# Row maxima of a block by four transfers for sixteen, and denominators inverted three steps later, in a mixed linear and softmax attention kernel

## The chip, the cores and the metric

One core of one Trainium2 chip runs the whole program. The metric is the device time of one execution in microseconds, the median of several runs.

## The reference

Two attention layers over the same input, mixed by a gate. Layer A is linear attention with a learned softmax feature map, layer B is ordinary softmax attention without a mask. There are 2048 tokens, a model width of 448, and 16 heads of 28.

```
q, k, v = split(x @ B_wqkv)                        # layer B
scores  = q @ k.T * 28 ** -0.5                     # 2048 x 2048 for each head
b = concat_heads(softmax(scores) @ v) @ B_wo
phi(u) = [softmax(u @ w_phi), softmax(-u @ w_phi)] # layer A
a = concat_heads(phi(q) (phi(k).T v) / (phi(q) sum(phi(k)) + 1e-6)) @ A_wo
g = sigmoid(sum(x * gate_w))
out = g * a + (1 - g) * b                          # all in fp32
```

The change concerns layer B, the softmax attention.

## The kernel before, in words

**Stages.** The first 360 us or so project q and k, compute layer A and the values of layer B, and begin the row maxima. After that comes the attention loop, 256 steps (`for s in range(NS + 18)`). The 16 heads lie in 4 groups of 4 (`g`), the queries in 4 ranges of 512 (`qb`). A block `gq = 4 * g + qb` is one group with one query range, and it takes 16 steps, one for each tile of 128 keys (`kt`). A step has 12 score matmuls (4 heads in 4 row strips of the TensorE array, 3 passes with high and low halves of q and k), 4 exponentials on ScalarE (L839) and, two steps later (`LAG`), 4 value matmuls (L976) that add into the one PSUM bank `pv`. Three more matmuls a step (L288) compute scores of later blocks for their row maxima, and VectorE reduces each of them (L295). Seven PSUM banks go round among these; the VectorE reduction of a step has to be done before its banks can be written again.

**Row maxima.** The softmax subtracts each query's maximum inside the score matmul. The query stack `qst` has, for each head, 32 partitions: row 32h holds the maxima, the 28 rows from 32h + 4 hold q. The key stack has -1 in that row. `mx_reduce` (L223) reduces a block's partial maxima to `red`, turns it in 32 x 32 squares on VectorE to `nm` (L234), and `load_nm` (L812) brings `nm` to the four rows of `qst` by small transfers (L817). `load_q` (L808, L804) brings q itself by four transfers. There are two query stacks, so those of block `gq + 2` can be filled when block `gq` has made its last scores.

**Denominators.** The values carry a column of ones, so row 32j + 28 of `pv` holds the denominators of head j. `finish` (L1012) works after a block's last step in parts that are listed by step in `late`:

- `f1`: VectorE copies `pv` to `oU` (L373), and SP spreads the denominators over 128 partitions, `den` (L376);
- `f2`: VectorE inverts them (L383), SP writes them to HBM, `rd` (L387), and reads them back broadcast over 32 partitions, `rs` (L388);
- `f3`: GpSimd multiplies `oU` by `rs` (L394); `f4`: it splits the result in two halves, `oT` (L402, L403);
- `f5`: SP stores `oT` to HBM (L1033) for the output projection. In the last group the projection reads `oT` itself (`project`, at the steps in `PROJ`).

`oU`, `oT` and `rs` have one buffer each here, `den` has two.

**Order.** The instructions of TensorE, VectorE, ScalarE and GpSimd stand in the order in which the program writes them. Those of SP, which issues every DMA, are put in order by the scheduler, by when it reckons them ready, and then run in that order: a transfer that waits holds up all behind it. SP often takes the loads of a stack long before the step that writes them down.

The names and lines below are those of the kernel before.

Of the kernel before, what the change touches and what calls it, by code (L numbers as in the profile page):

```python
# [8 lines left out]
F32 = mybir.dt.float32  # L9
F32R = mybir.dt.float32r  # L10
# [7 lines left out]
P = 128  # L18
# [5 lines left out]
NG = 4  # L24
# [12 lines left out]
def f32(ap):  # L37
    return ap.bitcast(F32)
# [3 lines left out]
def gated_mix_kernel(ctx, tc, xT, wqkB, wvB, wvA, wkAT, wqAT, phi, woA, woB,  # L42
# [7 lines left out]
    nc = tc.nc  # L50
# [5 lines left out]
    mxp = ctx.enter_context(tc.tile_pool(name="mxp", bufs=2))  # L56
# [100 lines left out]
    nm_of = {}  # L157
    acts = []
    subs = []
    part = mxp.tile([P, NU * 4], F32, name="part", bufs=1)  # L160
    nc.gpsimd.memset(part, LOWEST)
    red = mxp.tile([P, 32], F32R, name="red", bufs=1)
    nc.vector.memset(f32(red), 0.0)

    def take_acts():
# [57 lines left out]
    def mx_reduce(gq):  # L223

        col = 64 * gq
        n = 2 if gq < GM else 4

        def reduce():
            nc.vector.tensor_reduce(
                red[:, :16].rearrange("p (h t) -> p h t", t=4),  # L230
                part[:, col:col + 16 * n].rearrange("p (k t h) -> p h t k", t=4, h=4),
                AX.X, ALU.max)
            nm_of[gq] = nm = mxp.tile([P, 32], F32, tag="nm", name=f"nm{gq}", bufs=7)
            nc.vector.transpose(nm, f32(red))  # L234

        mxs["fin"].append(reduce)
# [132 lines left out]
    def normalize1(pool, pn, nm, n):  # L369

        oU = pool.tile([P, n, 512], F32, tag="oU", name=f"oU{nm}", bufs=2 * n - 1)
        for i in range(n):
            (nc.scalar.copy if n == 2 else nc.vector.tensor_copy)(oU[:, i, :], pn[i])  # L373
        den = pool.tile([P, n, 16], F32, tag="den", name=f"den{nm}", bufs=2)
        for i in range(n):
            nc.sync.dma_start(den[:, i, :], oU[DH:P:32, i, :])  # L376
        return oU, den

    def normalize2(pool, oU, den, nm, n, eps):

        if eps:
            nc.vector.tensor_scalar_add(den, den, EPS)
        nc.vector.reciprocal(den, den)  # L383
        rd = dr.tile([4, n * 512], F32, tag=f"rd{n}", name=f"rd{nm}", bufs=2)
        rs = pool.tile([P, n, 512], F32, tag="rs", name=f"rs{nm}", bufs=n)
        for k in range(n):
            nc.sync.dma_start(rd[:, k * 512:(k + 1) * 512], den[:, k, :])  # L387
        nc.sync.dma_start(rs.rearrange("p n q -> p (n q)"),  # L388
                          rd.unsqueeze(1).to_broadcast([4, 32, n * 512]))
        return oU, rs  # L390

    def normalize3(oU, rs, n):

        (nc.gpsimd if n == 1 else nc.vector).tensor_mul(oU, oU, rs)  # L394
        return oU

    def normalize4(pool, oU, nm, n):

        oTn = []
        for k in range(n):  # L400
            oT = pool.tile([P, 2, 512], F32R, tag="oT", name=f"oT{nm}_{k}", bufs=3 * n - 2)
            (nc.scalar.copy if n == 2 else nc.gpsimd.tensor_copy)(oT[:, 0, :], oU[:, k, :])  # L402
            nc.gpsimd.tensor_sub(oT[:, 1, :], oU[:, k, :], f32(oT[:, 0, :]))  # L403
            oTn.append(oT)
        return oTn
# [275 lines left out]
    for i in range(2 * NT + 11):  # L681
        t, q = i, i - NT
# [107 lines left out]
    qst_of, kst_of = {}, {}  # L790
# [20 lines left out]

    def load_nm(gq):  # L812
        nm = nm_of.pop(gq)
        for h in range(4):
            row = f32(qst_of[gq][32 * h:32 * h + 1, 0, :].rearrange("p (t b r) -> p t b r", b=4, r=32))
            for b in range(4):
                nc.sync.dma_start(row[:, :, b, :], nm[32 * b + 4 * h:32 * b + 4 * h + 4, :])  # L817

    def load_k(g, kb):
        kst_of[(g, kb)] = load_stack(kst[(4 * g + kb) % 5], k_d[g], kb * 512)  # L820
# [2 lines left out]
    pv_of, pts, late, mids = {}, {}, {}, {}  # L823
# [64 lines left out]
    stg = at  # L888
    load_q(0)
    load_nm(0)  # L890
    rlp = fr_s.enter_context(tc.tile_pool(name="rlp", bufs=1, reuse_waits="tile"))
    mx_unit()
# [88 lines left out]
    def project(qb, oT, tl):  # L981

        t = qb * 4 + tl
        acc = acc_of[qb][:, tl, :]
        po = take_bank(f"pob{t}")
        run(po[:, :D], first_passes(qb, tl) + out_passes(oT, tl * P, woB_s, NG - 1))
        nc.vector.scalar_tensor_tensor(acc, po[:, :D], gate1[:, t:t + 1], acc,  # L987
                                       op0=ALU.mult, op1=ALU.add)
        nc.sync.dma_start(out[0, t * P:(t + 1) * P, :], acc)
# [22 lines left out]
    def finish(gq, s):  # L1012

        st = {}
        g, qb = divmod(gq, NQ)
        last = gq == NG * NQ - 1

        def f1():
            st["n"] = normalize1(late_p, [pv_of[gq]], f"b{gq}", 1)

        def f2():
            st["n"] = normalize2(late_p, *st["n"], f"b{gq}", 1, False)

        def f3():
            st["n"] = normalize3(*st["n"], 1)

        def f4():
            st["o"], = normalize4(late_p, st["n"], f"b{gq}", 1)

        def f5():  # L1030
            for j in range(4):
                r = (4 * g + j) * DH
                nc.sync.dma_start(o_d[r:r + DH, :, qb * 512:(qb + 1) * 512],  # L1033
                                  f32(st["o"][32 * j:32 * j + DH]))

        if last:
            finish_last(gq)
            return
        copies.append(f1)
        late.setdefault(s + 3, []).append(f2)  # L1040
        late.setdefault(s + 7, []).append(f3)
        late.setdefault(s + 8, []).append(lambda: acts.append(f4))
        if g < NG - 1:
            late.setdefault(s + 13, []).append(f5)
        else:
            for tl in range(4):
                mids[PROJ[qb] + tl] = lambda tl=tl: project(qb, st["o"], tl)
# [57 lines left out]
    for s in range(NS + 18):  # L1105
        gq, kt = divmod(s, NT)
        g, qb = divmod(gq, NQ)
        take_acts()
        if s < NS:
            if s in (0, 3):  # L1110
                load_k(0, 2 + s // 3)
            if g + 1 < NG and qb == NQ - 1 and kt in (2, 7):
                load_k(g + 1, kt // 4)
            if g and qb == 0 and kt in (0, 2):
                load_k(g, 2 + kt // 2)
            if kt == 5 and gq + 1 < NG * NQ:
                load_q(gq + 1)
            if kt == (12 if gq + 1 < 14 else 14) and gq + 1 < NG * NQ - 1:
                load_nm(gq + 1)
            if s in OUTS:  # L1120
                load_out(OUTS.index(s))
            if g == NG - 1 and kt == (12 if qb < 2 else 14):
                load_acc(qb)
# [8 lines left out]
        while vals and vals[0] <= upto:  # L1132
            t = vals.pop(0)
            values(t)
            if t % NT == NT - 1:
                finish(t // NT, s)
        take_copies()
        mx_fin()
        if NG * NQ - 1 in nm_of and NG * NQ - 1 in qst_of:
            load_nm(NG * NQ - 1)  # L1140
# [70 lines left out]
```

## Time and profile before

| | us |
|---|---|
| median of 3 runs (lowest, highest) | 1004.69 (1003.24, 1008.66) |
| the profiled execution: time | 1004.62 |
| its span | 1002.8 |
| TensorE busy | 987.7 |
| ScalarE busy | 752.8 |
| VectorE busy | 725.6 |
| GpSimd busy | 234.2 |

The span runs from the first to the last instruction of the program; the other 1.8 us of the execution lie around it. [...] In the rows of a timeline stand the start and the duration in microseconds, the engine, the line and the operation, what it writes and reads, how many of them are merged in the row, and in square brackets the idle time before and what ended it. SPq is SP's queue of DMA issues: the duration there is that of the issue, not of the transfer. In the rows of waits stand the total, how often, and the longest.

### The profile page before, as it was taken

The numbers are of one execution on the slowest core, as the hardware profiler recorded it, in microseconds if no ns is written. First come the engines' busy times: TensorE is split into PE (matmuls) and PEld (weight loads), VectorE is DVE, ScalarE is ACT, GpSimd is POOL, SyncE is SP. The second block draws the span as 40 slices with busy tenths as digits, with TensorE's granted clock in tenths as the row PEclk, the third lists the DMA queues.
The fourth block names the chain that finished last, engine by engine and source line by source line (L and its number), as shares of the span: only waits on it lengthen the run. The fifth ranks groups of instructions, "written<-read, shape, count | busy, mean of one in ns | idle before, by whom it ended". The sixth has DMA issues, their size and how long they took to land.

```text
span 1002.8 us, 22531 instructions
## 1 busy us (share of the span) xinstructions
PE 987.7 (98%) x8392; PEld 604.5 (60%) x8392; DVE 725.6 (72%) x1335; ACT 752.8 (75%) x1442; POOL 234.2 (23%) x224
## 2 busy tenths in 40 slices
PE   9999999999999999999989999999999999999998
PEld 8877777877877655445544455545454555555555
DVE  5566777898765778888867888878877887885112
ACT  4455556587765789888878888898887888987662
POOL 1134544679634700201101101101011011100010
PEclk9999999999999999999999999999999999999999
DMA  8973010122233134211122121122221122100441
GB/s 305 313 236 111 32 53 32 43 57 79 80 105 103 64 117 137 51 47 49 49 85 67 41 60 43 46 76 79 68 81 40 50 75 73 31 20 12 148 156 56
DMA packets 56909, 84.49 MB, mean 84 GB/s; under 512 B 17984, under 2 KB 24752, under 8 KB 56800
## 3 DMA queue, kind: packets, MB, share of 16 engines
q1 hardware_dynamic: 56800, 83.06, 26.8%
q8 instruction: 66, 1.08, 0.4%
q14 instruction: 43, 0.35, 0.1%
HBM read 54.86 MB, written 27.78 MB: 82 GB/s over the span
## 4 chain that ended last, share of the span: by engine, by line
PE 86%; DVE 6%; DMA 3%; SPq 2%; issue 1%; ACT 1%; POOL 1%; DVEq 0%; POOLq 0%; ACTq 0%
PE g L831 27%; PE pv L976 24%; PE pqk L109 4%; PE pk L127 4%; PE poa L109 4%; PE pva L127 4%; PE g L288 3%; PE pob L109 3%; PE pmd L260 3%; PE pvb L127 2%; DVE part L295 2%; SPq L817 2%; DMA denb<-oUb 2%; PE pvb L109 1%; PE pq L109 1%
## 5 line engine op out<-in xcount | busy, mean ns | idle before, releaser
L839 ACT ACTIVATE p<-g 128x512 f32<-128x512 f32 x1020 | 526.1, 607 | 101.2 <-PE g L831 101.0
L295 DVE TENSOR_REDUCE part<-g 128x1 f32<-128x512 f32 x704 | 441.6, 682 | 82.9 <-PE g L288 80.5
L831 PEld LDWEIGHTS g<-qst,kst 32*128 32x128 f32 x3060 | 221.2, 184 | 226.9 <-DVE part L295 207.4
L831 PE MATMUL g<-qst,kst 32*128 32x512 f32 x3060 | 345.5, 423 | 8.9 <-DVE part L295 8.1
L976 PE MATMUL pv<-p,vb 128*32 128x512 f32 x2048 | 274.5, 608 | 0.0
L288 PE MATMUL g<-kc,qc 28*128 28x512 f32 x704 | 233.3, 496 | 0.5
L394 POOL TENSOR_TENSOR oUb<-oUb,rsb 128x512 f32<-128x512 f32 x15 | 19.3, 1285 | 526.5 <-DMA rsb<-rdb 314.5
L265 DVE CUSTOM_DVE_ANT_0 rl<-pmb,rl 128x512 f32<-128x512 f32 x160 | 103.2, 682 | 44.4 <-ACT rl L264 44.4
L264 ACT ACTIVATE rl<-pmd 128x512 f32<-128x512 f32 x160 | 87.3, 601 | 31.2 <-PE pmb L260 28.3
L288 PEld LDWEIGHTS g<-kc,qc 28*128 28x128 f32 x704 | 87.0, 183 | 3.0 <-DVE part L295 2.6
L976 PEld LDWEIGHTS pv<-p,vb 128*32 128x32 f32 x2048 | 40.6, 108 | 68.5 <-issue 67.3
L109 PE MATMUL pqk<-XH,wB 128*128 128x512 f32 x192 | 59.3, 397 | 0.0
L987 DVE SCALAR_TENSOR_TENSOR acc<-pob,gate,acc 128x448 f32<-128x448 f32 x12 | 8.2, 684 | 54.2 <-PE pob L109 54.2
L546 ACT CAST ev<-pqk 128x512 fp32r<-128x512 f32 x28 | 16.0, 588 | 37.5 <-PE pqk L109 23.9
L109 PE MATMUL poa<-woA_s,oTa 128*128 128x448 f32 x192 | 43.4, 375 | 0.0
L260 PE MATMUL pmb<-kp,qp 28*128 28x512 f32 x160 | 42.3, 493 | 0.5
L109 PEld LDWEIGHTS pqk<-XH,wB 128*128 128x128 f32 x192 | 35.3, 188 | 8.9 <-issue 1.5
L547 DVE TENSOR_TENSOR ev<-pqk,ev 128x512 fp32r<-128x512 f32 x28 | 19.0, 689 | 29.2 <-ACT ev L546 29.0
L260 PE MATMUL pmd<-kp,qp 28*128 28x512 f32 x160 | 40.0, 495 | 0.0
L127 PE MATMUL pk<-wkA_s,XH 128*128 128x448 f32 x128 | 39.4, 382 | 0.0
L109 PEld LDWEIGHTS poa<-woA_s,oTa 128*128 128x128 f32 x192 | 34.9, 188 | 6.3 <-issue 2.9
L127 PE MATMUL pva<-wvA_s,XH 128*128 128x450 f32 x128 | 37.8, 371 | 0.0
(154 smaller groups left out, 1084.5 us busy)
## 6 DMA issues: line engine op xcount, KB each, us to landing
qkd<-ev SPq DMA_DIRECT2D x28, 512.0 KB
qst<-qkd SPq DMA_DIRECT2D x64, 112.0 KB
kst<-qkd SPq DMA_DIRECT2D x64, 112.0 KB
od<-oTb SPq DMA_DIRECT2D x48, 112.0 KB
rsa<-rda SPq DMA_DIRECT2D x8, 512.0 KB
qst<-nm SPq DMA_DIRECT2D x256, 0.5 KB
oL<-od SPq DMA_DIRECT2D x8, 512.0 KB
rsb<-rdb SPq DMA_DIRECT2D x15, 256.0 KB
```

The lines of the kernel that those rows point to most:

```text
L109: nc.tensor.matmul(dst, l, r, start=i == 0, stop=i == len(todo) - 1)
L127: nc.tensor.matmul(dst[:, :n], l, r, start=i == 0, stop=i == len(todo) - 1, skip_group_check=True)
L260: nc.tensor.matmul(pm[j], qc[js, qt * P:(qt + 1) * P], kc[js, :], start=True, stop=True, tile_position=(32 * i, 0))
L264: nc.scalar.activation(rl, pm[i], AF.Relu)
L265: nc.vector.tensor_tensor_reduce(rl, pm[2 + i], rl, 1.0, LOWEST, ALU.add, ALU.max, part[:, col + i:col + i + 1])
L288: nc.tensor.matmul(pm, mxs[("qc", gq)][js, qt * P:(qt + 1) * P], mxs[("kc", gq // NQ, kb)][js, :], start=True, stop=True, tile_position=(3 ...
L295: nc.vector.tensor_reduce(part[:, col:col + 1], pm, AX.X, ALU.max)
L394: (nc.gpsimd if n == 1 else nc.vector).tensor_mul(oU, oU, rs)
L817: nc.sync.dma_start(row[:, :, b, :], nm[32 * b + 4 * h:32 * b + 4 * h + 4, :])
L831: nc.tensor.matmul(st[j], kst_of[(gq // NQ, kt // 4)][js, k, (kt % 4) * P:(kt % 4 + 1) * P], qst_of[gq][js, q, :], start=n == 0, stop=n == ...
L839: nc.scalar.activation(p, st[j], AF.Exp, scale=SCALE)
L976: nc.tensor.matmul(pv[32 * j:32 * j + 32, :], vb[kt // 8][:, kt % 8, 4 * g + j, :], pt[j], start=kt == 0, stop=kt == NT - 1, tile_position ...
```

## The change

The transposed maxima get another layout. `red` becomes 128 columns wide: the four maxima of tile t of the query range stand in columns 32t to 32t + 3, one for each head, and the other columns stay zero. The transpose then turns four squares of 32 columns, and a head's maxima of a 32-query square come to lie in one partition, 32b + h, for all four tiles. Four transfers, one for each square row b, bring four partitions each to the rows 0, 32, 64 and 96 of the query stack; there were sixteen, one for each head and square row. Each transfer moves 16 runs of 128 bytes, where it moved 4.

In `finish`, the steps `f2`, `f3` and `f4` come three steps later, except for the last two blocks, and `f5` comes two steps later.

```
-    red = mxp.tile([P, 32], F32R, name="red", bufs=1)
+    red = mxp.tile([P, 128], F32R, name="red", bufs=1)
...
             nc.vector.tensor_reduce(
-                red[:, :16].rearrange("p (h t) -> p h t", t=4),
-                part[:, col:col + 16 * n].rearrange("p (k t h) -> p h t k", t=4, h=4),
+                red.rearrange("p (t c) -> p t c", t=4)[:, :, :4],
+                part[:, col:col + 16 * n].rearrange("p (k t h) -> p t h k", t=4, h=4),
                 AX.X, ALU.max)
-            nm_of[gq] = nm = mxp.tile([P, 32], F32, tag="nm", name=f"nm{gq}", bufs=7)
+            nm_of[gq] = nm = mxp.tile([P, 128], F32, tag="nm", name=f"nm{gq}", bufs=7)
             nc.vector.transpose(nm, f32(red))
...
     def load_nm(gq):
         nm = nm_of.pop(gq)
-        for h in range(4):
-            row = f32(qst_of[gq][32 * h:32 * h + 1, 0, :].rearrange("p (t b r) -> p t b r", b=4, r=32))
-            for b in range(4):
-                nc.sync.dma_start(row[:, :, b, :], nm[32 * b + 4 * h:32 * b + 4 * h + 4, :])
+        row = f32(qst_of[gq][0:P:32, 0, :].rearrange("h (t b r) -> h t b r", b=4, r=32))
+        for b in range(4):
+            nc.sync.dma_start(row[:, :, b, :], nm[32 * b:32 * b + 4, :].rearrange("h (t r) -> h t r", t=4))
...
         copies.append(f1)
-        late.setdefault(s + 3, []).append(f2)
-        late.setdefault(s + 7, []).append(f3)
-        late.setdefault(s + 8, []).append(lambda: acts.append(f4))
+        by = 3 if g < NG - 1 or qb < 2 else 0
+        late.setdefault(s + 3 + by, []).append(f2)
+        late.setdefault(s + 7 + by, []).append(f3)
+        late.setdefault(s + 8 + by, []).append(lambda: acts.append(f4))
         if g < NG - 1:
-            late.setdefault(s + 13, []).append(f5)
+            late.setdefault(s + 15, []).append(f5)
```

## The prediction

> **What bounds the kernel now.** I read the page first, for the busy shares and the chain of waits.
>
> ```profile
> PE 987.7 (98%) x8392; PEld 604.5 (60%) x8392; DVE 725.6 (72%) x1335; ACT 752.8 (75%) x1442; POOL 234.2 (23%) x224
> ```
>
> ```profile
> PE 86%; DVE 6%; DMA 3%; SPq 2%; issue 1%; ACT 1%; POOL 1%; DVEq 0%; POOLq 0%; ACTq 0%
> ```
>
> TensorE is the bound, but the chain leaves it: it passes through DVE, a DMA and SP's queue, and those are the two things the diff edits. So the second view is the timeline of TensorE, for the pace of the attention steps. A step begins its value matmuls with one row of L976; these are the rows of step 0, step 208 and step 224 (blocks 0, 13 and 14).
>
> ```profile
> 362.76 1.07 PE L976 MATMUL pv<-p,vb 128*32 128x512 f32 x8
> ```
>
> ```profile
> 859.54 1.07 PE L976 MATMUL pv<-p,vb 128*32 128x512 f32 x8
> ```
>
> ```profile
> 896.31 1.07 PE L976 MATMUL pv<-p,vb 128*32 128x512 f32 x8
> ```
>
> Block 13 takes 896.31 - 859.54 = 36.77 us, 2.298 us a step. At that pace the 14 blocks from 362.76 would take 14 x 36.77 = 514.8 us; they take 896.31 - 362.76 = 533.55. So 18.8 us are lost in them somewhere. The third view, the waits, says where DVE stood.
>
> ```profile
> DVE denb L383 <- DMA denb<-oUb: 20.8, 12, 6.0
> ```
>
> ```profile
> SPq L1033 <- POOL oTb L403: 74.2, 10, 8.0
> ```
>
> The reciprocal of the denominators waits 12 times, 20.8 us in all, for the small transfer denb. That is the size of the loss. (The second row, SP's own, is used below.) The fourth view is the worst case, the denominators of block 3, inverted in block 4: first SP's queue, then DVE, POOL and TensorE in the same stretch.
>
> ```profile
> 482.20 3.56 SPq L804 DMA_DIRECT2D kst<-qkd  x4
> 485.86 0.47 SPq L387 DMA_DIRECT2D rdb<-denb  x1
> 488.24 0.58 SPq L388 DMA_DIRECT2D rsb<-rdb  x1
> 496.89 3.37 SPq L1033 DMA_DIRECT2D od<-oTb  x4
> 500.36 6.96 SPq L804 DMA_DIRECT2D kst<-qkd  x8
> 507.42 6.12 SPq L176 DMA_DIRECT2D kc<-qkd  x12
> 513.64 3.50 SPq L804 DMA_DIRECT2D qst<-qkd  x4
> 517.18 4.75 SPq L817 DMA_DIRECT2D qst<-nm  x7
> 522.04 0.60 SPq L376 DMA_DIRECT2D denb<-oUb  x1
> ```
>
> ```profile
> 481.60 0.25 DVE L383 RECIPROCAL denb<-denb 128x16 f32<-128x16 f32 x1 [0.86 <-DMA denb<-oUb]
> ...
> 511.01 0.69 DVE L373 COPY oUb<-pv 128x512 f32<-128x512 f32 x1
> ...
> 523.95 0.25 DVE L383 RECIPROCAL denb<-denb 128x16 f32<-128x16 f32 x1 [6.02 <-DMA denb<-oUb]
> ```
>
> ```profile
> 493.55 1.28 POOL L394 TENSOR_TENSOR oUb<-oUb,rsb 128x512 f32<-128x512 f32 x1 [36.05 <-DMA rsb<-rdb]
> 494.90 0.61 POOL L402 CAST oTb<-oUb 128x512 fp32r<-128x512 f32 x1
> 495.59 1.28 POOL L403 TENSOR_TENSOR oTb<-oUb,oTb 128x512 fp32r<-128x512 f32 x1
> ```
>
> ```profile
> 519.23 1.07 PE L976 MATMUL pv<-p,vb 128*32 128x512 f32 x8
> ...
> 527.57 1.94 PE L976 MATMUL pv<-p,vb 128*32 128x512 f32 x8
> ...
> 531.24 1.06 PE L976 MATMUL pv<-p,vb 128*32 128x512 f32 x8
> ```
>
> The copy that feeds denb is done at 511.7, but SP issues denb only at 522.04, behind query loads and seven of the sixteen row transfers; it lands 1.91 us later. DVE has reached the reciprocal at 523.95 - 6.02 = 517.93 and holds the next steps' L295 reductions behind it, these hold the PSUM banks, and TensorE has no bank to score into: two steps take 531.24 - 519.23 = 12.01 us in place of 4.60, so this one wait costs 7.4 us.
>
> Part of that is the clock. Windows over this place and over a shorter gap in block 10 (the third column from the right is the granted clock), then TensorE's gap and two step rows of block 10:
>
> ```profile
> 524.00:528.00 4.00, 3.20 (x19) 1.61 (x23) 3.49 (x7) 1.11 (x3) 0.00 (x0) 0.51 0.03 5
> 753.70:757.30 3.60, 3.42 (x26) 1.03 (x27) 3.01 (x5) 1.80 (x4) 0.00 (x0) 0.85 0.12 35
> 757.30:760.40 3.10, 3.10 (x27) 1.37 (x23) 1.98 (x3) 1.64 (x4) 0.62 (x1) 0.62 0.13 46
> ```
>
> ```profile
> 753.70 0.50 PE L831 MATMUL g<-qst,kst 32*128 32x512 f32 x2 [1.66 <-DVE part L295]
> ```
>
> ```profile
> 755.79 1.57 PE L976 MATMUL pv<-p,vb 128*32 128x512 f32 x8
> 759.30 1.20 PE L976 MATMUL pv<-p,vb 128*32 128x512 f32 x8
> ```
>
> After the stall the clock falls to 0.51, and in block 10 to 0.62, where the step after the wait takes 759.30 - 755.79 = 3.51 us, 1.21 over pace. I count it to the wait and let it go with it.
>
> **The change part by part.** *Sixteen row transfers become four.* The old ones (four runs of 128 bytes each) cost SP 4.75 / 7 = 0.68 us apiece, 10.9 us a block. A new one moves four times as many runs. The nearest rows: kc, 28 runs, 6.12 / 12 = 0.51 us; qst, 56 longer runs, 3.50 / 4 = 0.88 us. So issue time hardly follows the runs; I take 0.68, 2.7 us a block, with 0.51 as lower end and 4 x 0.68 = 2.7 us each (proportional to runs) as upper end. SP is nobody's bound, so the 8.2 us saved count only through denb. The rows land a block ahead of use, so nothing waits for them sooner or later.
>
> *Where denb then stands.* In the built program SP's order is: query loads (4), rows (4), denb, in most blocks; in block 4 two qc loads come between, in block 8 four qc and one kst, in block 9 one kc. Before, eleven rows (seven in block 4) stood ahead. Block 4 again, by rows: the reciprocal of block 2's denominators has its turn at 481.60 - 0.86 = 480.74, and three steps later at 487.6; rdb goes at 488.0, rsb 2.4 later (488.24 - 485.86) at 490.4, lands 5.3 later (493.55 - 488.24) at 495.7, POOL's three operations take 496.87 - 493.55 = 3.3, to 499.0, od 3.5, to 502.5. Then four kst (the other four of the eight now stand ahead of rsb) to 506.0, twelve kc to 512.2, four qst to 515.8, four rows to 518.5, two qc to 519.5, denb lands at 521.4.
>
> *The reciprocal three steps later.* Its turn moves from 517.93 by 6.9 to 524.8, or 524.0 if block 3's wait of 0.86 goes too. So even here denb is 2.6 us early, and elsewhere by more. The waits on denb go to none; what is late next is nothing on DVE, only TensorE's own pace of 2.298. Term: -18.8 us.
>
> *What moves with it.* POOL's multiply, cast and subtraction (steps 7 and 8 to 10 and 11), rdb and rsb after the reciprocal, and the four od stores. They hide behind POOL's idle time (36.05 us ahead of the multiply). The buffer oU must be free at the next block's copy, 511.01; it is free at 499.0, some 11 us early. Project steps (qb 0 and 1) come 24 and 16 steps after a block's end; block 14 isn't moved. Cost 0.
>
> *The wider transpose and reduction.* Sixteen of each:
>
> ```profile
> L229 DVE TENSOR_REDUCE red<-part x16: 129/252/266, 111.2 to 918.2; 128x16 fp32r<-128x64 f32 x11, 128x16 fp32r<-128x32 f32 x5
> L234 DVE STREAM_TRANSPOSE nm<-red x16: 211/211/214, 111.5 to 918.5; 128x32 f32<-128x32 f32 x16
> ```
>
> The reduction handles the same elements: 0. The transpose takes 128 columns for 32: between 0 and 3 x 0.211 = 0.63 us more. Nearest is the copy, 0.69 / 512 = 1.35 ns a column: 96 x 1.35 = 0.13 us. In the attention steps that is hidden, since DVE takes a whole copy of 0.69 without TensorE losing a step:
>
> ```profile
> 398.28 0.69 DVE L373 COPY oUb<-pv 128x512 f32<-128x512 f32 x1
> ```
>
> ```profile
> 399.47 1.07 PE L976 MATMUL pv<-p,vb 128*32 128x512 f32 x8
> ```
>
> ```profile
> 401.74 1.06 PE L976 MATMUL pv<-p,vb 128*32 128x512 f32 x8
> ```
>
> (The step right after the copy: 2.27 us.) The five of the earlier stage I count in full, 5 x 0.13 = +0.65; with all sixteen at the upper end it would be +10.1.
>
> Sum: 1004.62 (the profiled execution: span 1002.8 and 1.8 around it; the median of the three runs, 1004.69, is the same within 0.1) - 18.8 + 0.65 = 986.5.
>
> [...]
>
> **The rivals.** *The slow step stays.* If the clock of block 10 fell for another reason than its gap, 1.21 us remain: 987.7. Against: the low clock begins at the gap's end, in both blocks. It lies inside the forecast's own range, and I give it 0.05.
>
> *Issue goes by runs.* At 2.7 us a row transfer, denb of block 4 lands 8.1 us later, at 529.5, 5 us behind the reciprocal, and the place costs nearly what it costs now, 7.4: 993.9. For it: 56-run loads take longer than 28-run ones. Against: 14 times the runs of an old row transfer cost 1.3 times as much.
>
> *The transpose is slow and seen*: +10.1 less 0.65, 996. Against it speaks the hidden copy.
>
> *Slower: oU is held too long.* The three steps come off its slack. If rsb landed over 11 us later than I work out, DVE's copy would wait for POOL, the one pv bank would stay full, and every later step of TensorE would wait. For it: SP blocks on L1033 for oT already (74.2 us, up to 8.0), and rdb and rsb stand behind kst loads in that in-order queue. Against: denb, the latest of these transfers, is 6.0 us late at worst now. At one step in each of 13 blocks it costs 13 x 2.3 = 29.9: 1016. It decides from 18.8 / 13 = 1.4 us of copy wait a block; around that point the result is no change, about 1005.
>
> **How the numbers follow.** A change under 0.5% (5.0 us) can't be told from none here. Forecast 0.75 (own range 984 to 990); the slow step 0.05, in the same range; issue by runs 0.08 and transpose 0.04, both still faster; oU about at break-even 0.03; oU beyond 0.05. So faster 0.92, same 0.03, slower 0.05. Low end: the transposes hidden, 985.9, less the 1.45 by which the fastest run lies under the median, about 984. High end: issue by runs at 993.9, so 994.5. That leaves out the slow transpose and the oU cases, 0.12.
>
> **What would show it.** In the profile after: the wait of L383 for denb gone or under 2 us in all; steps of 2.30 throughout blocks 1 to 12, none at 8 or 4; the granted clock 1.0 in them; four row transfers a block at 0.5 to 0.9 us each; transposes near 0.34 us. Wrong would be: row transfers of 2 us or more and a wait left in block 4; a wait of L373 for POOL; or steps still over pace with no wait on denb, which would mean that the loss was never denb's.

## The result and the profile after

The changed kernel takes 987.08 us (median of 6 runs, 986.0 to 988.71) against 1004.35 (6 runs, 1002.64 to 1008.66). The ratio is 0.983, with a 95% interval of 0.981 to 0.985. 986.5 was forecast.

The page of the changed kernel, its busy shares and its chain. From the row transfers on, a line's number is lower by one here: the row transfers are L816 (L817 before), and L830, L838, L975 and L1032 are L831, L839, L976 and L1033 of before.

```profile
PE 979.2 (99%) x8392; PEld 607.2 (62%) x8392; DVE 728.5 (74%) x1335; ACT 752.9 (76%) x1442; POOL 234.8 (24%) x224
```

```profile
PE 95%; DVE 3%; issue 1%; ACT 0%; POOL 0%; DVEq 0%; POOLq 0%; ACTq 0%
```

The chain no longer leaves TensorE for SP's queue or a DMA: DMA and SPq, 5% of the chain before, are gone from it. TensorE's busy time fell by 8.5 us though it does the same work: rows such as block 4's value matmuls of 1.94 us, in a window granted 0.51 of the clock, are gone. The longest of the 2048 value matmuls takes 618 ns here; it took 1062 ns before.

The same three step rows as before (steps 0, 208 and 224; the last two are taken from narrow windows, which hold only the first 4 of the row's 8 matmuls, and only their starts are used):

```profile
362.25 1.07 PE L975 MATMUL pv<-p,vb 128*32 128x512 f32 x8
```

```profile
841.01 0.64 PE L975 MATMUL pv<-p,vb 128*32 128x512 f32 x4
```

```profile
877.80 0.64 PE L975 MATMUL pv<-p,vb 128*32 128x512 f32 x4
```

Block 13 takes 36.79 us, as before (36.77). The 14 blocks take 877.80 - 362.25 = 515.55 us, against 533.55: 18.0 us less. The span lost 17.8 in all (1002.8 to 985.0), so the rest of the program evens out to 0.2.

The place of the worst wait, SP and DVE around block 4:

```profile
496.10 3.35 SPq L1032 DMA_DIRECT2D od<-oTb  x4
499.49 3.48 SPq L804 DMA_DIRECT2D kst<-qkd  x4
503.07 6.43 SPq L176 DMA_DIRECT2D kc<-qkd  x12
509.60 3.47 SPq L804 DMA_DIRECT2D qst<-qkd  x4
513.12 2.37 SPq L816 DMA_DIRECT2D qst<-nm  x4
515.59 0.83 SPq L176 DMA_DIRECT2D qc<-qkd  x2
516.52 0.58 SPq L376 DMA_DIRECT2D denb<-oUb  x1
```

```profile
508.18 0.68 DVE L373 COPY oUb<-pv 128x512 f32<-128x512 f32 x1
...
521.85 0.24 DVE L383 RECIPROCAL denb<-denb 128x16 f32<-128x16 f32 x1
```

The reciprocal's row has no bracket: DVE came to it and went on. denb left SP 5.3 us ahead of the reciprocal, 7.7 us after the copy's end; it had been 10.3. The wait of L383 for denb, 20.8 us in 12 waits before, is not in the list of waits any more.

SP itself now waits longer. The broadcast chain stands behind a later reciprocal:

```profile
SPq L387 <- DVE denb L383: 67.4, 9, 11.4
```

That was 8.9 us in two waits. What stands behind rdb in the queue, key loads among it, is held up as long; no engine's wait for those loads has come into the list.

### The profile page after: what moved, and what is told of

It is laid out like the page before. It is cut to its first block, busy times and chain, and to the rows that moved or that the text cites. A ratio compares the mean times of both kernels' runs of the same rounds, so it can differ in the third digit from the quotient of the medians.

```text
span 985.0 us, 22282 instructions
## 1 busy us (share of the span) xinstructions
PE 979.2 (99%) x8392; PEld 607.2 (62%) x8392; DVE 728.5 (74%) x1335; ACT 752.9 (76%) x1442; POOL 234.8 (24%) x224
## 4 chain that ended last, share of the span: by engine, by line
PE 95%; DVE 3%; issue 1%; ACT 0%; POOL 0%; DVEq 0%; POOLq 0%; ACTq 0%
PE g L830 29%; PE pv L975 26%; PE pqk L109 6%; PE poa L109 4%; PE pk L127 4%; PE pva L127 4%; PE g L288 3%; PE pmd L260 3%; PE pob L109 3%; PE pvb L127 2%; PE pvb L109 2%; PE pq L109 2%; PE pn L507 1%; PE pqk L608 1%; PE pft L495 1%
## 5 line engine op out<-in xcount | busy, mean ns | idle before, releaser
L838 ACT ACTIVATE p<-g 128x512 f32<-128x512 f32 x1020 | 526.1, 607 | 83.9 <-PE g L830 83.1
L830 PEld LDWEIGHTS g<-qst,kst 32*128 32x128 f32 x3060 | 221.2, 183 | 212.1 <-DVE part L295 194.6
L830 PE MATMUL g<-qst,kst 32*128 32x512 f32 x3060 | 337.9, 420 | 0.1
L975 PE MATMUL pv<-p,vb 128*32 128x512 f32 x2048 | 273.0, 605 | 0.0
L394 POOL TENSOR_TENSOR oUb<-oUb,rsb 128x512 f32<-128x512 f32 x15 | 19.3, 1286 | 490.5 <-DMA rsb<-rdb 458.4
L975 PEld LDWEIGHTS pv<-p,vb 128*32 128x32 f32 x2048 | 40.7, 108 | 65.9 <-issue 64.6
```

The source lines that it names most:

```text
L830: nc.tensor.matmul(st[j], kst_of[(gq // NQ, kt // 4)][js, k, (kt % 4) * P:(kt % 4 + 1) * P], qst_of[gq][js, q, :], start=n == 0, stop=n == ...
L838: nc.scalar.activation(p, st[j], AF.Exp, scale=SCALE)
L975: nc.tensor.matmul(pv[32 * j:32 * j + 32, :], vb[kt // 8][:, kt % 8, 4 * g + j, :], pt[j], start=kt == 0, stop=kt == NT - 1, tile_position ...
```

## The experiments

### The changed kernel once more

Run beside the next three on one chip.

> The changed kernel as it is, run beside the three variants that follow so that they are compared on one chip: 986 to 989 us, no wait of the reciprocal for denb.

Measured: 987.33 us (986.51 to 989.04), ratio to before 0.981 (0.979 to 0.983). The next three are read against it.

### Only the four wide transfers

```
-        by = 3 if g < NG - 1 or qb < 2 else 0
+        by = 0
...
-            late.setdefault(s + 15, []).append(f5)
+            late.setdefault(s + 13, []).append(f5)
```

(The diff is against the changed kernel.)

> Only the four wide row transfers; the reciprocal stays at three steps after a block's end. Theory (the loss is the reciprocal waiting for denb, and nothing else): in all blocks but two SP is idle when the copy is done, so denb goes at once, lands 2 us later and the reciprocal, 6.2 us after the copy, finds it there. In block 4 the eight kst and twelve kc loads still stand ahead: SP reaches denb at about 520.6 on the time scale of before, it lands at 522.5 against a turn of 517.9, a wait of 4 to 5 us, worth 5 to 6.5 us of time. About 992 us. Rival (what pays is SP's shorter queue, and the later reciprocal is of no account): 987 us as the full change, no wait left. Rival (the parts pay half each): 995 us.

Measured: 987.15 us (986.79 to 988.03), ratio 0.981 (0.978 to 0.983). That is the full gain, and 5 us less than I expected of the theory. No wait for denb was left. SP's queue of this kernel before block 4, and its DVE, show where the working missed:

```profile
490.74 3.35 SPq L1032 DMA_DIRECT2D od<-oTb  x4
494.19 7.22 SPq L804 DMA_DIRECT2D kst<-qkd  x8
501.51 5.19 SPq L176 DMA_DIRECT2D kc<-qkd  x12
506.80 3.81 SPq L804 DMA_DIRECT2D qst<-qkd  x4
510.66 2.39 SPq L816 DMA_DIRECT2D qst<-nm  x4
513.15 0.83 SPq L176 DMA_DIRECT2D qc<-qkd  x2
514.08 0.59 SPq L376 DMA_DIRECT2D denb<-oUb  x1
```

```profile
509.26 0.67 DVE L373 COPY oUb<-pv 128x512 f32<-128x512 f32 x1
...
516.09 0.24 DVE L383 RECIPROCAL denb<-denb 128x16 f32<-128x16 f32 x1
```

I had left the stores of the block before (od) at their old time, 496.89. They come at 490.74, because that block's own denb, reciprocal and broadcast had gone earlier too. Measured from that block's copy they come 5 us earlier than before, the loads behind them as well, and denb goes 4.2 us after its copy. At 514.08 plus the 1.9 us that landing took before, it is there when the reciprocal is due, at 516.09, with nothing to spare. A prediction that shortens one part of an in-order queue has to shorten every cycle of it, not the last one alone.

Once this is mended, the theory and the rival "SP's shorter queue pays" both say 987 here, so this run doesn't tell them apart; the next two do.

### Only the later reciprocal

The steps of the changed kernel, with the sixteen narrow transfers of the kernel before.

> Only the later steps: the reciprocal six steps after a block's end, POOL's work and the stores as in the changed kernel; sixteen narrow row transfers as before. Theory (the wait for denb is the loss): the longest wait of before, 6.02 us in block 4, is shorter than three steps, 6.9 us, so no wait is left anywhere: 985.5 to 988 us, the same as the full change. Rival (SP's queue pays by itself): above 995 us. Rival (half each): 995 us.

Measured: 986.5 us (986.09 to 987.77), ratio 0.980 (0.977 to 0.982). One wait is left, in block 5:

```profile
DVE denb L383 <- DMA denb<-oUb: 1.2, 1, 1.2
```

The sixteen transfers are all there, denb leaves SP 5 to 12 us after the copy in blocks 1 to 12, and the time is that of the full change. I had expected no wait at all, because the longest of before, 6.02 us, was shorter than three steps. But the later steps move SP's queue too: in block 5 denb leaves SP 12.4 us after the copy's end, where the latest before was 10.3, and the three steps fall 1.2 us short there. So SP's shorter queue pays nothing by itself; what pays is that denb is there before the reciprocal's turn. Each part does that alone, the later steps all but for that 1.2 us. Together they gain what one gains, some 18 us, and not the sum.

### Neither part, but denb on another queue

```
-            nc.sync.dma_start(den[:, i, :], oU[DH:P:32, i, :])
+            (nc.gpsimd if n == 1 else nc.sync).dma_start(den[:, i, :], oU[DH:P:32, i, :])
```

(Against the kernel before.)

> Neither part of the change: the kernel before, but the small transfer denb of the attention blocks is issued by GpSimd in place of SP, so that it stands behind no row transfers. Theory (denb is late because it stands behind SP's queue): it goes when the copy is done, lands well within the 6.2 us that the reciprocal leaves, and the waits go: 986 to 990 us, if GpSimd's issue and landing take under 6 us together. Rival (the transfer itself is slow, or the time is lost for another reason at these steps): 1000 to 1005 us, waits as before.

Measured: 986.93 us (985.6 to 987.73), ratio 0.980 (0.978 to 0.982), no wait for denb. The denominators of block 3 in this run, first GpSimd's issue, then DVE:

```profile
508.69 0.69 POOL L376 DMA_DIRECT2D denb<-oUb  x1 [15.19 <-DVE oUb L373]
```

```profile
514.53 0.24 DVE L383 RECIPROCAL denb<-denb 128x16 f32<-128x16 f32 x1
```

GpSimd had waited for the copy alone, and the transfer took 2.3 us from issue to landing in the median of the 15. With the old transfers, the old steps and one instruction on another queue, the 18 us are gone too. That settles the cause: denb's place in SP's in-order queue, behind the row transfers and, in block 4 above all, behind loads as well.

### The reciprocal too late

This is the prediction's rival that ends slower, taken to its edge: the changed kernel with the reciprocal later still, against GpSimd's hold on the one buffer oU.

```
+        far = g < NG - 1
-        late.setdefault(s + 3 + by, []).append(f2)
-        late.setdefault(s + 7 + by, []).append(f3)
-        late.setdefault(s + 8 + by, []).append(lambda: acts.append(f4))
+        late.setdefault(s + (12 if far else 3 + by), []).append(f2)
+        late.setdefault(s + (14 if far else 7 + by), []).append(f3)
+        late.setdefault(s + (15 if far else 8 + by), []).append(lambda: acts.append(f4))
...
-            late.setdefault(s + 15, []).append(f5)
+            late.setdefault(s + 16, []).append(f5)
```

> The changed kernel, but in the first three groups the reciprocal comes twelve steps after a block's end, POOL's multiply and split fourteen and fifteen, the stores sixteen. Theory (the one rival that ends slower is real, and its edge is where oU is held past the next copy): from the reciprocal to the end of oT it is 10.2 us in the changed kernel; with the reciprocal 26.9 us after the copy, oT ends 37.1 us after it, and the next copy's turn is 36.1 us after it. DVE's copy then waits for POOL about 1 us a block, more where the broadcast is held up by loads (block 3: 3 us): 12 to 18 us over twelve blocks, 999 to 1005 us in all. Rival (oU's slack is longer than worked out, or the copy can wait unseen): 987 us.

> As the kernel with twelve steps, but thirteen. Theory: one step, 2.3 us, more of waiting in each of twelve blocks: 25 to 28 us over the kernel with twelve steps, 1025 to 1032 us, the wait of the copy for POOL at 3.3 us. Rival: 987 us, or no more than a few us over the kernel with twelve steps.

Measured: with twelve steps 1004.46 us (1002.63 to 1007.12), ratio to before 0.997 (0.994 to 0.999): nearly all of the gain is given back. With thirteen (12 becomes 13 in the first line) 1064.21 us (1063.39 to 1065.91), ratio 1.056 (1.053 to 1.060).

TensorE's wait with twelve steps, and DVE's with thirteen:

```profile
PE pv L975 <- DVE oUb L373: 11.6, 12, 2.7
```

```profile
DVE oUb L373 <- POOL oTb L403: 57.4, 12, 5.2
```

The edge lies where it was worked out: twelve waits of TensorE, 1 us each on average and 2.7 at the longest. They are not the whole price: TensorE's busy time rises too, from 979.2 us in the changed kernel to 985.6. Beyond the edge the price was more than twice what I expected, 60 us for one step. TensorE's wait for the copy grows by 40.7 us (11.6 to 52.3) and its busy time, for the same work, by 19.3 (985.6 to 1004.9). Two things that I had left out are seen in the rows. First, oT comes later than the step alone explains: for the denominators of block 1 the broadcast rsb is issued at 473.32 with query loads right behind it, and GpSimd's multiply starts 7.0 us later; with twelve steps it is 464.93 and 470.61, 5.7 us.

```profile
473.32 0.56 SPq L388 DMA_DIRECT2D rsb<-rdb  x1
474.00 2.97 SPq L804 DMA_DIRECT2D qst<-qkd  x3
```

```profile
480.32 1.27 POOL L394 TENSOR_TENSOR oUb<-oUb,rsb 128x512 f32<-128x512 f32 x1 [30.58 <-DMA qst<-qkd]
```

Second, TensorE's gap of 4.71 us, which ends at 484.38, right behind that copy, costs clock. These are windows of the kernel with thirteen steps; behind the length stands TensorE's busy time, and the third column from the right is the granted clock.

```profile
482.00:484.00 2.00, 0.00 (x0) 0.00 (x0) 0.36 (x1) 0.00 (x0) 1.52 (x2) 0.74 0.00 0
484.00:488.00 4.00, 3.62 (x23) 1.38 (x23) 2.98 (x6) 0.01 (x1) 0.00 (x0) 0.50 0.43 88
488.00:491.00 3.00, 3.00 (x26) 0.90 (x23) 1.53 (x3) 2.06 (x4) 0.00 (x0) 0.70 0.21 44
```

### The reciprocal too early

```
-        late.setdefault(s + 3 + by, []).append(f2)
+        late.setdefault(s, []).append(f2)
```

(Against the changed kernel.)

> The changed kernel, but the reciprocal stands right behind the copy of its block, so that DVE waits for denb's own issue and landing, about 2 us, in nearly every block. Theory (TensorE loses what DVE waits, less the 0.7 us or so that the banks absorb): copy 0.69, wait 2.0 and reciprocal 0.25 less 0.74 is 2.2 us in ten blocks, more in four where loads stand ahead: 35 to 45 us, 1022 to 1032 us, if the clock holds. If TensorE's clock falls after each such gap, as the rows of block 10 suggested, some 1.2 us a block come on top: 1037 to 1050 us, and the granted clock of these stretches lies under 0.9. Rival (the reciprocal's wait was never what TensorE lost): 987 us.

Measured: 1037.47 us (1034.78 to 1038.15), ratio to before 1.029 (1.025 to 1.032). That is 50 us over the changed kernel by the times, 46 by the ratios (the two were measured on different chips).

```profile
DVE denb L383 <- DMA denb<-oUb: 34.4, 15, 4.2
```

```profile
PE g L830 <- DVE part L295: 22.4, 14, 3.6
```

The wait is back in every block, 1.91 to 2.07 us in most, and with it the loss. The theory without the clock fell short, and that with the clock in every block was at its lower end: the clock falls behind nine of TensorE's fourteen gaps. Windows of two blocks with nearly the same gap, 1.19 us ending at 400.76 and 1.31 us ending at 439.69:

```profile
398.00:402.00 4.00, 2.62 (x26) 0.84 (x20) 2.09 (x5) 2.09 (x5) 0.00 (x0) 1.00 0.04 4
402.00:405.00 3.00, 3.00 (x32) 1.57 (x32) 2.33 (x4) 2.16 (x5) 0.00 (x0) 1.00 0.18 63
437.00:441.00 4.00, 2.51 (x25) 0.72 (x22) 2.16 (x5) 2.06 (x4) 0.00 (x0) 1.00 0.04 4
441.00:444.00 3.00, 3.00 (x25) 1.22 (x29) 1.70 (x3) 2.07 (x4) 0.00 (x0) 0.71 0.18 53
```

Against the changed kernel the first block lost 2.0 us, the second 3.5. A step of normal length follows the first gap; a step of 3.45 us follows the second.

## Why the prediction was right, step by step

- **The size of the loss.** Worked out as 18.8 us from TensorE's pace; 18.0 came back. The 14 blocks take 0.8 us more than the 14 x 36.77 = 514.8 that was worked out. Some of it is in two steps of 2.6 and 2.5 us in blocks 6 and 10, which I have not traced. That the loss was the reciprocal's wait for denb, and not something that falls on the same steps, was argued; the run with denb on GpSimd's queue shows it.
- **Block 4.** denb was to leave SP 7.8 us after the copy's end and land 2.6 us ahead of the reciprocal. It left 7.7 us after it, and with the 1.9 us that landing took before, it was about 3.4 us early.
- **The term for the later reciprocal, -18.8.** Right in size, wrong as an account of the parts: I charged the whole gain to the three steps and let the transfers count only through denb's place. The transfers alone bring the same 18 us, and so do the steps alone. My expectation for the transfers alone (992) failed at one step, the store time of the block before, as shown there.
- **Row transfers.** 0.68 us apiece was taken, 2.7 a block. They take 2.37 / 4 = 0.59. Four times the runs cost SP nothing: the median issue is 552 ns, where the narrow one's was 573. The rival "issue goes by runs" is out.

```profile
L816 SPq DMA_DIRECT2D qst<-nm x64: 537/552/752, 336.3 to 902.2; - x64
```

- **The wide transpose.** I took 0.34 us from the copy's rate; it takes 0.311, exactly 0.100 more than the narrow one (0.211). That is 1.04 ns for each of the 96 columns more, where the copy's rate gave 1.35. Whether the five of the earlier stage cost any time can't be read: the loop starts at 362.25 us, and before at 362.76.

```profile
L234 DVE STREAM_TRANSPOSE nm<-red x16: 311/311/313, 111.6 to 900.1; 128x128 f32<-128x128 f32 x16
```

- **oU.** It was to be free some 11 us ahead of the next copy; by the prediction's own figures, 511.01 - 499.0, it is 12.0. In block 3 the stores, which wait for GpSimd's last operation, are issued at 496.10 and the copy starts at 508.18: 12.1 us. The rival that ends slower is real, and six steps away, as the run with twelve steps shows.
- **The clock.** I let the slow step of block 10 go with its gap. It went: a window over 740 to 760 us, all in block 10, is granted 1.00, where 757.30 to 760.40 was granted 0.62 before. A short gap can lower the clock, but need not: it was 0.71 behind one of 1.31 us in the run with the reciprocal too early, and 1.00 behind one of 1.43 us in the kernel before (the last section has its rows).

```profile
740.00:760.00 20.00, 20.00 (x204) 10.51 (x198) 16.56 (x30) 18.10 (x36) 3.18 (x3) 1.00 0.19 49
```

## What to carry to other kernels

In a queue that runs in order, look at what stands ahead of the one small transfer that an engine waits for; its delay is theirs, not its own (in block 4 of before denb left SP 10.3 us after the copy and took 1.9 us to land). Several edits that each bring it ahead of its deadline gain the same time once (some 18 us here, by either part or by both), so test them apart before adding up. And a consumer moved later takes its slack from a buffer's release: work out that edge too, for behind it one step of 2.3 us cost 5 us a block here.

## What the hardware showed unasked

A short gap in TensorE's work sometimes lowers its clock and sometimes doesn't, and in the run with the reciprocal too early the length of the gap does not decide it. That run has 12 gaps of 1.19 to 1.51 us, and two longer ones; the first two, as TensorE's rows show them (the gap stands in brackets, and ends where the row begins):

```profile
400.76 0.49 PE L830 MATMUL g<-qst,kst 32*128 32x512 f32 x2 [1.19 <-DVE part L295]
```

```profile
439.69 0.50 PE L830 MATMUL g<-qst,kst 32*128 32x512 f32 x2 [1.31 <-DVE part L295]
```

Behind the first, the window from 402 to 405 us is granted 1.00, behind the second the one from 441 to 444 us 0.71. In the table, of the 12 gaps, the clock held where no value matmul behind the gap took over 617 ns, and fell where some took 1033 to 1062 ns.

```
gap starts at (us)
clock held:  399.57 478.67 560.49 724.37 884.92
clock fell:  438.38 599.33 640.14 763.32 804.08
             844.42 923.81
```

The lengths of the two groups overlap: one gap of 1.34 us held, and one of 1.25 fell. The kernel before, in another run, has a gap of 1.43 us behind which the clock held. Its row, and the windows from its end on:

```profile
677.51 0.50 PE L831 MATMUL g<-qst,kst 32*128 32x512 f32 x2 [1.43 <-DVE part L295]
```

```profile
677.50:680.00 2.50, 2.31 (x19) 1.02 (x23) 2.50 (x5) 0.69 (x2) 0.00 (x0) 1.00 0.32 92
680.00:684.00 4.00, 4.00 (x46) 2.22 (x38) 2.96 (x5) 3.53 (x8) 0.00 (x0) 1.00 0.41 117
```

What decides was not found: neither the length of a gap nor the time at which it falls was varied by itself.
